# One transformer block on one core: the search for the order of its operations takes another seed and 73 rounds for 110

## The chip, the cores and the metric

The kernel runs on one core of one Trainium2 chip. That core has five engines that work side by side, each through its own list of instructions in order: TensorE (PE in the profile, with PEld for its weight loads), VectorE (DVE), ScalarE (ACT), GpSimd (POOL) and SyncE (SP), which here issues the DMA transfers. An instruction waits until what it reads has been written and what it overwrites has been read.

The metric is the time of one execution on the device in microseconds (us), the median of several runs. All times below are us from the start of the profiled span unless they say otherwise.

## The reference, cut to what matters

One sequence of 2048 tokens with 448 features goes through one block: layer norm, attention with 16 heads of 28 in a sliding window of 256 tokens, a residual addition, layer norm, a gated feed-forward part of width 1792, and a second residual addition.

```python
h = x + attention(layernorm(x))          # 16 heads, Dh 28
    # q, k, v = split(y @ wqkv);  p = softmax(mask(q @ k.T * 28 ** -0.5)), 0 <= i - j < 256
    # (p @ v) @ wo
h2 = h + (gelu(y @ w_gate) * (y @ w_up)) @ w_down      # y = layernorm(h), width 1792
return h2                                               # all float32
```

## The kernel before, in words

**Numbers.** Products in float32 are made from two parts: the high part of a value (`to_hi`, line 498, an ACT copy into the matmul type) and the rest (`to_lo`, line 501, a subtraction on DVE or POOL). A projection, a value product or a feed-forward convolution is then a sum of hi x hi, hi x lo and lo x hi. So nearly every matmul has line 495 (the helper `mul`); which one it is, the names of its operands and its width tell.

**Stages.** Tokens are cut into 16 tiles of 128 and 4 chunks of 512. The heads are worked on in two passes of 8. In each pass and chunk the kernel makes

- values: 11 matmuls of width 224 per tile (`bank<-proj,xT 128x224`), evicted by ACT;
- projections of queries and keys: 11 matmuls of width 512 per weight tile (`bank<-xT,proj 128x512`); their result goes to DRAM and comes back into `ring` in the layout of the scores;
- two blocks of four heads and 512 queries, 16 in all. A block has 16 scores (`bank<-ring` 84x384, one per head and query tile); DVE takes the masked row maximum of each from its PSUM bank (line 924, tile `mt`); for each half of the block one small matmul (line 951, `one,mhl`) turns the maxima, which ACT writes beside the queries; then 24 probability matmuls (`bank<-ring` 104x128 to 104x384) give the scores again, transposed and with the maximum subtracted, and ACT takes the exponential out of the bank (line 996, tile `pp`); POOL clears what lies outside the window (line 1007). Two attention groups per block (line 1026, twelve matmuls each, recorded as 24, `bank<-pp,v`) multiply by the values; 32 of them in all;
- the output projection: 24 matmuls per chunk (`bank<-wos,ohl 128x448`), added to the residual `hres` by DVE (line 1073).

The feed-forward part starts with eight plain convolution steps (line 1320 issues them; the first two, 'early', are made while attention still runs and have the form `bank<-xT,proj 128x512` too), and goes on with 24 steps in a scheme of seven products each (`unit`), whose operands POOL and DVE form (line 693 and line 1164). Each step is followed by a down projection into four banks, which DVE adds to `hres` (line 1296). Weight records for it come in by DMA (line 1157, `raw<-in_halves`) and are split into `proj` or `ring`. The transposed operands go by way of small transfers (line 674, `v<-xn`).

**Banks.** PSUM has eight banks. Two take scores, two probabilities, two are the attention accumulators, and the last two take values, projections and output products, and scores or probabilities once the projections are done (`allowed`, line 1533). A matmul into a bank waits until the engine that evicts it is through with the result before.

**What sets the order.** Nothing is issued as it is written. Each operation is recorded by `op` with its engine, an assumed cost, a latency, a key, and what it reads and writes. `run` (line 140) then plays the lists through: at each step it takes, among the operations that are ready on an engine, the one with the lowest key that can begin soonest, gives it a bank if it needs one, and so forms one list per engine. Where PE would have nothing in the first 26 us, `idle` puts a transpose of the identity there (line 1571).

Before that, `refine` (line 337) changes the keys. It draws from a random generator with a fixed seed. In each round it either sets all keys from the latest times at which the operations could run without delaying the end (`latest`, line 290), mixed with their present times and with noise, or shifts the operations of one kind in one stretch. Then it plays the lists anew and values the order with

```python
return 1e9 if s is None else 0.4 * s + 0.3 * sum(self.replay(random.Random(i)) for i in (1, 2))
```

where `s` is the end by the assumed costs and `replay` (line 252) plays the fixed order with costs that are longer at random. A better order is kept, a worse one with a probability that falls. The keys of the best order found are those that are used:

```python
L.refine(allowed, idle)
L.run(allowed, idle, True)
```

Of the kernel before, what the change touches and what calls it, by code (L numbers as in the profile page):

```python
# [72 lines left out]
    return max(n / 2400 + 0.004, 0.112)  # L73


ROUNDS = 110
SEED = 3
HEAT = 0.3
MIX = 0.8
COOL = 800  # L80
# [16 lines left out]
class Lists:  # L97
# [239 lines left out]
    def refine(self, allowed, idle):  # L337

        rnd = random.Random(SEED)

# [5 lines left out]
        kept = keys = [o.key for o in self.ops]  # L346
        for r in range(ROUNDS):
            kind = rnd.random()
# [1285 lines left out]
```

## Time and profile before

| what | value |
|---|---|
| median of 3 runs | 686.99 us (686.92 to 687.37) |
| the profiled execution | 687.41 us |
| its span | 685.70 us, so 1.71 us lie around it |
| mean granted clock of TensorE | 0.998 |
| starts of attention groups 22 to 32 | 230.08, 239.57, 248.45, 258.52, 266.00, 273.71, 286.00, 292.87, 304.17, 311.02, 319.36 |
| share of the span on the chain of work that ended last | PE 86%, DVE 7%, ACT 3%, DMA 3% |

A row of the timeline has the start, the length, the engine, the line, the operation and its operands (destination <- sources, partitions x elements), and a count where like instructions were joined; what stands in brackets is the idle time ahead of it and what ended that. A row of the windows has the stretch, its length, then for PE, PEld, DVE, ACT and POOL the busy time and the number of instructions, and at the end the granted clock (1.00 is full speed), the share of the DMA engines' time that was busy, and GB/s. Matmuls overlap their neighbours, so the distance from one start to the next is shorter than a recorded length.

### The profile page before, as it was taken

The page shows a single profiled execution, that of the slowest core. Times are in us where ns is not written, and L with a number is a line of the kernel's source. Part 1 is how long each engine was busy: PE and PEld are TensorE (multiplying, and loading weights), DVE is VectorE, ACT ScalarE, POOL GpSimd, SP SyncE. Part 2 cuts the span into 40 slices and gives each one's busy share as a digit, 9 for nine tenths or more (in the row PEclk, how much of TensorE's full clock was granted, in tenths as well). Part 3 has the DMA queues.
Part 4 walks back from the last instruction along what each step waited for, and adds up shares of the span by engine and source line. Part 5 has one row for each costly group of instructions (what it writes and reads, how often), then busy time and mean ns, then how long its engine had stood idle before and what let it go on. Part 6 is the DMA issues. An engine that isn't in the chain of part 4 may idle for free.

```text
span 685.7 us, 12258 instructions
## 1 busy us (share of the span) xinstructions
PE 673.9 (98%) x4079; PEld 593.4 (87%) x4079; DVE 502.4 (73%) x1274; ACT 419.6 (61%) x908; POOL 296.8 (43%) x462
## 2 busy tenths in 40 slices
PE   8999999999999999999999999999999999999997
PEld 8898888888888877677898899899999999999997
DVE  7968978866587867784899998877667745645544
ACT  7758767777766789696655665644554543533331
POOL 5702544344445668546524465254664631501100
PEclk9999999999999999999999999999999999999999
DMA  8798765566547687633533432212212210111102
GB/s 290 229 307 264 225 186 177 165 191 197 174 149 221 171 245 195 168 74 85 148 91 101 116 110 75 86 53 76 66 53 90 67 53 14 39 53 67 54 1 107
DMA packets 92951, 89.67 MB, mean 131 GB/s; under 512 B 35224, under 2 KB 82008, under 8 KB 92888
## 3 DMA queue, kind: packets, MB, share of 16 engines
q1 hardware_dynamic: 92888, 88.89, 43.4%
q8 instruction: 32, 0.52, 0.3%
q14 instruction: 31, 0.25, 0.1%
HBM read 59.51 MB, written 29.36 MB: 130 GB/s over the span
## 4 chain that ended last, share of the span: by engine, by line
PE 86%; DVE 7%; ACT 3%; DMA 3%; issue 1%; POOL 0%; SPq 0%; DVEq 0%; ACTq 0%
PE bank L495 79%; PE bank L1026 6%; DMA v<-xn 1%; ACT ring L498 1%; PE bank L553 1%; DVE proj L501 1%; DVE v L693 1%; DVE X L501 1%; DVE mt L924 1%; DVE hres L1296 1%; DMA q<-proj 1%; ACT proj L498 1%; ACT xT L498 1%; ACT pp L996 1%; DVE bnst L530 0%
## 5 line engine op out<-in xcount | busy, mean ns | idle before, releaser
L495 PE MATMUL bank<-xT,proj 128*128 128x512 f32 x620 | 178.9, 387 | 0.0
L495 PE MATMUL bank<-ring 84*128 84x384 f32 (+5 forms) x618 | 155.4, 314 | 2.6 <-ACT pp L996 1.5
L924 DVE CUSTOM_DVE_ANT_0 mt<-bank,mt 128x384 bf16<-128x384 f32 (+2 forms) x256 | 129.0, 526 | 36.9 <-PE bank L495 31.9
L996 ACT ACTIVATE pp<-bank 128x384 f32<-128x384 f32 (+2 forms) x352 | 123.6, 390 | 45.1 <-PE bank L495 41.7
L495 PE MATMUL bank<-xT,ring 128*128 128x512 f32 x536 | 134.9, 380 | 0.1
L495 PEld LDWEIGHTS bank<-ring 104*128 104x128 f32 (+2 forms) x618 | 109.8, 191 | 25.6 <-issue 5.6
L495 PE MATMUL bank<-ring,proj 128*128 128x448 f32 x628 | 127.5, 353 | 1.6 <-DVE hres L1296 1.6
L1007 POOL TENSOR_SCALAR_AFFINE_SELECT pp<-pp 128x512 f32<-128x512 f32 x120 | 74.9, 638 | 117.2 <-ACT pp L996 106.1
L495 PEld LDWEIGHTS bank<-xT,proj 128*128 128x128 f32 x620 | 114.4, 191 | 10.8 <-issue 0.6
L495 PEld LDWEIGHTS bank<-ring,proj 128*128 128x128 f32 x628 | 118.6, 189 | 4.6 <-ACT xT L498 1.9
L495 PEld LDWEIGHTS bank<-xT,ring 128*128 128x128 f32 x536 | 100.9, 189 | 13.5 <-DVE v L1240 0.5
L1296 DVE TENSOR_TENSOR hres<-bank,hres 128x448 f32<-128x448 f32 x72 | 41.3, 622 | 26.8 <-PE bank L495 26.7
L495 PE MATMUL bank<-proj,xT 128*128 128x224 f32 x352 | 59.9, 275 | 0.2 <-ACT proj L498 0.2
L1258 ACT ACTIVATE v<-v 128x512 f32<-128x512 f32 x24 | 15.2, 632 | 69.5 <-DVE v L1240 69.5
L501 POOL TENSOR_TENSOR ring<-raw,ring 128x256 fp32r<-128x256 f32 (+2 forms) x42 | 38.3, 921 | 42.1 <-ACT ring L498 34.3
L495 PEld LDWEIGHTS bank<-proj,xT 128*128 128x128 f32 x352 | 53.2, 191 | 1.5 <-ACT proj L498 0.4
L1164 POOL TENSOR_TENSOR v<-raw 128x256 f32<-128x256 f32 x18 | 15.4, 856 | 89.8 <-DMA raw<-in_halves_dram 54.9
L495 PE MATMUL bank<-wos,ohl 128*128 128x448 f32 x192 | 50.2, 363 | 0.0
L501 DVE TENSOR_TENSOR proj<-v,proj 128x512 fp32r<-128x512 f32 (+1 forms) x56 | 43.0, 773 | 8.6 <-ACT proj L498 7.4
L498 ACT ACTIVATE proj<-v 128x512 fp32r<-128x512 f32 (+1 forms) x56 | 33.6, 603 | 24.3 <-DVE v L1266 13.4
L495 PE MATMUL bank<-X,ring 128*128 128x512 f32 x146 | 48.2, 379 | 0.0
L1164 POOL TENSOR_TENSOR raw<-raw 64x128 f32<-64x128 f32 (+1 forms) x90 | 46.1, 525 | 2.2
(116 smaller groups left out, 987.5 us busy)
## 6 DMA issues: line engine op xcount, KB each, us to landing
ring<-k SPq DMA_DIRECT2D x44, 336.0 KB
raw<-in_halves_dram SPq DMA_DIRECT2D x18, 640.0 KB
ring<-q SPq DMA_DIRECT2D x32, 336.0 KB
q<-proj SPq DMA_DIRECT2D x15, 448.0 KB
k<-proj SPq DMA_DIRECT2D x11, 448.0 KB
hres<-in_x_dram SPq DMA_DIRECT2D x16, 224.0 KB
xn<-xn SPq DMA_DIRECT2D x64, 56.0 KB
mt<-in_halves_dram SPq DMA_DIRECT2D x16, 224.0 KB
```

Of the source, the lines that this page charges most:

```text
L495: nc.tensor.matmul(o.rearrange("p (t h) -> p t h", h=2), w, mixed(m), **how)
L498: nc.scalar.activation(dst, src, AF.Copy)
L501: (eng or nc.vector).tensor_sub(dst, src, f(hi))
L553: nc.tensor.transpose(bank[b.k][:, n * 128:(n + 1) * 128], xn[i2][:, o:o + 128], ident)
L693: op("dve", 0.07 + n * 0.00104, 0.17 + n * 0.00104, key, lambda: nc.vector.tensor_tensor(out, a, b, op=op_), [*ar, *br, "mtfree"], w, port ...
L924: nc.vector.tensor_tensor_reduce(plain(junk[s % 2][:, o:384]), unmixed(bank[b.k][:, o:384]), plain(mask[:, o:384]), 1.0, -BIG, OP.add, OP. ...
L996: nc.scalar.activation(plain(pp[:, j, o * 128:o * 128 + n]), unmixed(bank[b.k][:, 0:n]), AF.Exp, scale=SCALE)
L1007: nc.gpsimd.affine_select(a, a, pattern=[[0, 4], [-cm, 128]], compare_op=op_, fill=0.0, base=0, channel_multiplier=cm)
L1026: nc.tensor.matmul(bank[b.k][32 * j:32 * j + DH + 1, lo * 128:(hi + 1) * 128], v[:, 4 * c - 2 + m, g % 2, j, :], pp[:, j, at[m] * 128:(at[ ...
L1164: op("pool", 0.14 + n * 0.00215, 0.18 + n * 0.00215, key, lambda: nc.gpsimd.tensor_tensor(out, a, b, op=OP.subtract), [*ar, *br], w, port= ...
L1258: op("act", 0.485, 0.608, key + 11, lambda: nc.scalar.activation(A, A, AF.Gelu_apprx_tanh), ta, ta)
L1296: op("dve", 0.533, 0.626, key + 3 * q + 3, lambda t=t, b=banks[q]: nc.vector.tensor_tensor(plain(hres[:, t, :]), unmixed(bank[b.k][:, 0:D] ...
```

## The change

Two constants of the search differ:

```diff
-ROUNDS = 110
-SEED = 3
+ROUNDS = 73
+SEED = 13
 HEAT = 0.3
 MIX = 0.8
 COOL = 800
```

The operations, their operands, their costs and what depends on what are the same. What differs is the random sequence, so other keys are tried, and the order that comes out is another. The warming transposes go from 35 to 38. PE's list differs up to the matmul that stands at 329.10 in the profile before, and is the same from there to the end (1696 operations); DVE and ACT differ up to about 440, POOL and SP up to about 500.

Three places show it. The names `bank_138` to `bank_145` are the eight PSUM banks: 138 and 139 take scores (384 wide), 140 and 141 probabilities, 142 and 143 are the accumulators of attention, 144 and 145 the two shared ones.

The first place is PE behind attention group 25. Before, from the fourth row behind the group on:

```order
L495 MATMUL bank_144<-wos,ohl 128x448
L495 MATMUL bank_145<-ring 128x256
L495 MATMUL bank_144<-wos,ohl 128x448
L951 MATMUL bank_141<-one,mhl_156 72x128
L495 MATMUL bank_144<-wos,ohl 128x448
L495 MATMUL bank_138<-ring 128x384
L495 MATMUL bank_140<-ring 128x128
L495 MATMUL bank_144<-wos,ohl 128x448
L495 MATMUL bank_139<-ring 128x384
L495 MATMUL bank_145<-ring 128x256
```

And now, from the first row behind the same group:

```order
L495 MATMUL bank_140<-ring 128x256
L495 MATMUL bank_144<-wos,ohl 128x448
L495 MATMUL bank_141<-ring 128x256
L495 MATMUL bank_144<-wos,ohl 128x448 x4
L495 MATMUL bank_140<-ring 128x256
L495 MATMUL bank_144<-wos,ohl 128x448
L495 MATMUL bank_141<-ring 128x256
L495 MATMUL bank_145<-ring 128x128
L495 MATMUL bank_138<-ring 128x384
L495 MATMUL bank_140<-ring 128x128
L495 MATMUL bank_141<-ring 128x128
L495 MATMUL bank_144<-wos,ohl 128x448 x6
```

Between groups 25 and 26 the output matmuls (`wos,ohl`) were 12 and are 24 now, all four tiles of the chunk, and two value matmuls stand there too. The scores in this stretch were 6 and there is 1. Counted over all from group 22 to group 32, value matmuls were 54 and are 66, projections 28 and 33, output matmuls 48 and 53; scores 63 and 62; probabilities (115), early convolutions (71) and turned maxima (9) are as many as before.

The second place is PE and ACT behind attention group 27. PE before, from the end of the group on:

```order
L1026 MATMUL bank_143<-pp,v 29x384 x4
L495 MATMUL bank_138<-ring 128x384
L495 MATMUL bank_139<-ring 128x384
L495 MATMUL bank_140<-ring 128x256
L495 MATMUL bank_141<-ring 128x256
L495 MATMUL bank_145<-ring 128x128
L495 MATMUL bank_140<-ring 128x256
L495 MATMUL bank_141<-ring 128x128
L495 MATMUL bank_138<-ring 128x384
```

PE now:

```order
L1026 MATMUL bank_143<-pp,v 29x384 x4
L495 MATMUL bank_140<-ring 128x384
L495 MATMUL bank_138<-ring 128x384
L495 MATMUL bank_141<-ring 128x256
L495 MATMUL bank_139<-ring 128x384
L495 MATMUL bank_145<-ring 128x256
L495 MATMUL bank_140<-ring 128x256
L495 MATMUL bank_138<-ring 128x384
L495 MATMUL bank_141<-ring 128x256
L495 MATMUL bank_145<-ring 128x384
```

ACT in the same place now:

```order
L498 ACTIVATE v<-bank_144 128x8x28
L498 ACTIVATE ohl<-oT 128x512
L498 ACTIVATE proj<-raw 128x512 x2
L996 ACTIVATE pp<-bank_140 128x384
L996 ACTIVATE pp<-bank_141 128x256
L996 ACTIVATE pp<-bank_145 128x256
L498 ACTIVATE xT<-xT 128x3x128
L498 ACTIVATE ring<-xT 64x128
L498 ACTIVATE xT<-xT 64x128
L996 ACTIVATE pp<-bank_140 128x256
L996 ACTIVATE pp<-bank_141 128x256
L498 ACTIVATE proj<-raw 128x448
```

Behind the group 17 scores and probabilities stand ahead of the first early convolution before and now, in another sequence. On ACT three splits of a weight record (`proj<-raw`) now stand between this group and the next, where there was none before.

The third place is DVE at the second group of four residual additions of the feed-forward part (line 1296; PE takes the same four banks again behind them). Before:

```order
L693 TENSOR_TENSOR v<-v 128x128
L1341 TENSOR_TENSOR mt<-bank_139,mt 128x512
L1296 TENSOR_TENSOR hres<-bank_142,hres 128x448
L1296 TENSOR_TENSOR hres<-bank_143,hres 128x448
L1296 TENSOR_TENSOR hres<-bank_144,hres 128x448
L1296 TENSOR_TENSOR hres<-bank_145,hres 128x448
```

Now:

```order
L501 TENSOR_TENSOR proj<-raw,proj 128x2x128 x2
L1296 TENSOR_TENSOR hres<-bank_142,hres 128x448
L1296 TENSOR_TENSOR hres<-bank_143,hres 128x448
L1296 TENSOR_TENSOR hres<-bank_144,hres 128x448
L1296 TENSOR_TENSOR hres<-bank_145,hres 128x448
L1341 TENSOR_TENSOR mt<-bank_139,mt 128x512
```

The product with the gate (line 1341) has gone behind the four additions, and one more split (line 501) stands ahead of them. On SP the load of a weight record (line 1157) that stood ahead of a run of transfers `v<-xn` stands behind three of them now.

## The prediction

> **What bounds the kernel now.** I read the page's head, the waits of PE, the busy time by stage, the same table between attention groups, and last the timeline of single places. The page first:
>
> ```profile
> span 685.7 us, 12258 instructions
> PE 673.9 (98%) x4079; PEld 593.4 (87%) x4079; DVE 502.4 (73%) x1274; ACT 419.6 (61%) x908; POOL 296.8 (43%) x462
> ```
> PE (TensorE) is busy for all but 11.8 us of the span. A new order leaves the matmuls as they are, so it can only take waits out or put waits in. The waits that PE's engine shows (engine, line, waited for; total, times, longest):
>
> ```profile
> PE bank L495 <- DVE proj L501: 1.7, 1, 1.7
> PE bank L495 <- DVE hres L1296: 1.6, 1, 1.6
> PE bank L495 <- ACT pp L996: 1.5, 4, 0.8
> PE bank L495 <- DVE mx L924: 0.6, 2, 0.4
> ```
> Two are single places; the others are small and belong to one stretch. The table by stage (start:end, length, then busy us of PE, PEld, DVE, ACT, POOL with counts, granted clock, DMA) shows which:
>
> ```profile
> 12.00:25.00 13.00, 13.00 (x82) 11.70 (x81) 12.45 (x31) 12.34 (x23) 8.83 (x23) 1.00 0.66 230
> 25.00:230.08 205.08, 205.03 (x1553) 176.28 (x1551) 160.68 (x552) 146.56 (x366) 85.41 (x120) 1.00 0.67 206
> 230.08:319.36 89.28, 86.64 (x630) 67.92 (x629) 64.81 (x205) 75.22 (x196) 57.62 (x86) 0.98 0.64 160
> 331.10:365.40 34.30, 32.71 (x160) 30.02 (x160) 31.13 (x84) 19.54 (x35) 11.19 (x20) 1.00 0.40 109
> 398.80:680.40 281.60, 281.60 (x1372) 259.04 (x1373) 183.32 (x310) 131.45 (x234) 102.73 (x160) 1.00 0.19 59
> ```
> From 12 to 230.08 us and from 398.80 to 680.40 us PE never lets go for more than 0.05 us in all. The waits stand in 230.08:319.36 (attention groups 22 to 32), where the clock is below 1 as well, and at the two handovers behind it. Busy time hides part of a wait, since a matmul's recorded time overlaps the next one's; so I price matmuls by the distance of their starts:
>
> ```profile
> 249.86 0.81 PE L495 MATMUL bank<-ring 84*128 84x384 f32 x4
> 250.51 1.03 PE L495 MATMUL bank<-xT,proj 128*128 128x512 f32 x4
> 251.38 0.28 PE L495 MATMUL bank<-ring 104*128 104x256 f32 x1
> 251.49 0.23 PE L951 MATMUL bank<-one,mhl 128*72 128x128 f32 x1
> ...
> 251.77 0.48 PE L495 MATMUL bank<-proj,xT 128*128 128x224 f32 x3
> 252.09 0.34 PE L495 MATMUL bank<-ring 84*128 84x384 f32 x1
> ...
> 273.71 1.50 PE L1026 MATMUL bank<-pp,v 128*29 128x128 f32 x24
> 275.14 0.88 PE L495 MATMUL bank<-ring 84*128 84x384 f32 x5
> ...
> 324.56 4.70 PE L495 MATMUL bank<-wos,ohl 128*128 128x448 f32 x24
> 329.10 0.35 PE L495 MATMUL bank<-proj 128*128 128x448 f32 x1
> ```
> A score of 384 columns costs 0.65/4 = 0.16 us, a projection or early conv of 512 0.87/4 = 0.22, a probability of 256 0.11 (0.06 for 128 by halving; 0.11 on the average of a block's 24), a value matmul 0.32/3 = 0.11, an output matmul 4.54/24 = 0.19. An attention group takes 1.43 us (273.71 to 275.14), and I allow 0.5 us for its start and end (an estimate: with it the sums below come out at no wait for the stretches where PE's row is full).
>
> **The stretch with the waits.** One row from each group to the next:
>
> ```profile
> 239.57:248.45 8.88, 8.77 (x77) 7.33 (x77) 4.88 (x17) 7.83 (x23) 5.78 (x8) 1.00 0.89 250
> 248.45:258.52 10.07, 9.32 (x76) 7.76 (x75) 7.48 (x24) 8.30 (x22) 6.19 (x9) 1.00 0.89 245
> 258.52:266.00 7.48, 7.22 (x56) 5.36 (x55) 5.79 (x22) 6.39 (x20) 5.15 (x7) 1.00 0.94 242
> 266.00:273.71 7.71, 7.53 (x55) 5.55 (x54) 5.56 (x16) 7.16 (x19) 7.22 (x13) 1.00 0.62 152
> 273.71:286.00 12.29, 11.24 (x69) 8.20 (x69) 9.40 (x37) 7.68 (x23) 7.45 (x12) 0.86 0.83 215
> 286.00:292.87 6.87, 6.87 (x55) 5.15 (x54) 5.99 (x19) 5.72 (x14) 3.69 (x6) 1.00 0.31 67
> ```
> With the order's counts at the prices above, PE's own work from group 27 to group 28 (273.71:286.00) is 7.7 us (the group, 13 scores, 16 probabilities, 11 early convs, one maximum); with the 0.5 us around the group 4.1 us are waits. The same sum gives 1.6 us for 248.45:258.52, 0.9 for 258.52:266.00, 0.7 for 266.00:273.71 and for 239.57:248.45, 0 for 286.00:292.87, and 0.8 us for the stretches not shown: 8.8 us for the ten from group 22 to group 32. What the 4.1 us are:
>
> ```profile
> 276.32 0.60 PE L495 MATMUL bank<-ring 104*128 104x256 f32 x2 [0.30 <-ACT pp L996]
> 277.31 1.63 PE L495 MATMUL bank<-ring 84*128 84x384 f32 x6 [0.40 <-DVE mx L924]
> 279.17 0.91 PE L495 MATMUL bank<-ring 84*128 84x384 f32 x3 [0.22 <-DVE mx L924]
> 279.91 1.44 PE L495 MATMUL bank<-xT,proj 128*128 128x512 f32 x4
> ...
> 281.00:282.00 1.00, 1.00 (x4) 0.76 (x3) 0.26 (x2) 0.50 (x1) 0.91 (x3) 0.50 0.98 275
> ...
> L924 DVE CUSTOM_DVE_ANT_0 mt<-bank,mt 128x384 bf16<-128x384 f32 (+2 forms) x256 | 129.0, 526 | 36.9 <-PE bank L495 31.9
> ```
> Behind group 27 stand 17 scores and probabilities without any filler (a matmul that waits for no bank of the block); they take 4.77 us for 2.4 us of work, since each score needs 0.53 us of DVE before its bank comes back. Then the clock falls to 0.50, which costs the other 1.7 us or so.
>
> **Term 1, the fillers, -1.8 us.** From group 22 to group 32 the new order has 12 value, 5 projection and 5 output matmuls more (66, 33, 53 against 54, 28, 48) and as many scores, probabilities and early convs: 12 x 0.11 + 5 x 0.22 + 5 x 0.19 = 3.4 us of work that stood ahead of group 22, where PE did not wait. So group 22 comes 3.4 us earlier, the work behind it is 3.4 us more, and only the waits count. Groups 25 to 26: 26 fillers in place of 12, so that 0.9 falls to 0.2. Groups 26 to 27: 20 for 12, but of the shorter kind; 0.7 falls to 0.2. Groups 24 to 25: 22 for 26, and the last ten in front of the group are scores, probabilities and a maximum; five scores take 2.6 us of DVE beside 1.3 us of PE, of which half may be covered: 1.6 falls to 0.9 (ends 0 and 1.6). Groups 27 to 28: again 17 small matmuls before the first early conv; 4.1 stays, the half-speed clock with it (ends 2.4 without it and 5.8 with a second one). The rest stays. The sum of waits is 6.9 us in place of 8.8 (the shares rounded to -1.8).
>
> [...]
>
> **Term 2, the handovers, -0.3 us.** At 365.4 PE waits for the four residual additions that give the down banks back:
>
> ```profile
> 364.02 0.68 DVE L1341 TENSOR_TENSOR mt<-bank,mt 128x512 f32<-128x512 f32 x1
> 364.63 2.20 DVE L1296 TENSOR_TENSOR hres<-bank,hres 128x448 f32<-128x448 f32 x4
> ```
> The new order puts the 0.6 us of L1341 behind them and a split of 0.33 us ahead: the additions come 0.27 us earlier. What is late next is that L1341, whose result the down group two steps on reads, some 7 us later. At 331.1 PE waits 1.7 us for the low part of the first conv product. In the run of DVE in front of it the same four additions, three products and one statistic stand in another order, and one transpose of 0.64 us has left it, which lay ahead of a wait:
>
> ```profile
> 325.89 0.62 DVE L1073 TENSOR_TENSOR hres<-bank,hres 128x448 f32<-128x448 f32 x1 [0.48 <-PE bank L495]
> ```
> I take 0 (ends -0.6 and +0.6, one operation either way).
>
> **Term 3, the rest, +0.1 us.** From 329.1 us on PE's own order is the same to the end. DVE, ACT and SP change up to 500 us, under 281.60 us in which DVE is busy for 183.32: this cover holds unless one result comes late by more than its margin. The largest move is on SP:
>
> ```profile
> 363.10 0.36 SPq L1157 DMA_DIRECT2D raw<-in_halves_dram  x1
> 363.51 7.41 SPq L674 DMA_DIRECT2D v<-xn  x6
> ...
> 377.39 0.41 DVE L501 TENSOR_TENSOR ring<-raw,ring 128x256 fp32r<-128x256 f32 x1
> ...
> 379.49 1.03 PE L495 MATMUL bank<-xT,ring 128*128 128x512 f32 x4
> ```
> The weight record's load now stands behind three of those six, up to some 4 us later (363.51 and half of 7.41, against 363.10). Its last split ended at 377.80, and PE reads it from the third matmul of the row at 379.49, 379.9: a margin of 2.1 us. Ends 0 and +2; I take 0.1, nearest the rows without a wait. At the start three more warming transposes (38 for 35) fill waits and cost nothing; the first projection is bound by the same DVE work up to about 14 us, and from 12 us on the table shows no wait (ends -0.5 and +0.5).
>
> The sum is -2.0 us. The profiled execution took 687.41 us (span 685.70 and 1.71 around it), 0.42 above the median of 686.99; against the median the forecast is 685.0 us.
>
> **The rivals.** [...] (b) No gain: the pace in groups 24 to 28 is set by the chain score, maximum, probability, exponential, and fillers only shift the waits: 687.0. For it: no engine is full there (DVE 7.48 of 10.07, ACT 8.30). (c) Slower: ACT sets the pace. Between groups 24 and 28 the new order gives ACT 30.0 us up to the last exponential needed, against 27.5, and three weight splits of 0.6 us stand between the exponentials for group 28. For it: ACT is 7.16 of 7.71 busy in 266.00:273.71 and ended four waits. Then this stretch takes 37.6 + 2.5 us, from a start 2.0 us earlier, PE has 0.6 us more to do behind group 28, so +1.1; a second half-speed stretch brings +1.7, and terms 2 and 3 -0.2: 689.6. It decides where ACT falls over 2 us behind PE at group 28. Against it: ACT had room of 4.6 us in 273.71:286.00. That the order stays as it was is excluded: it differs on every engine.
>
> **How the numbers follow.** 0.2% is 1.4 us, about what a measurement of this kernel can tell from no change. Forecast 0.45, own range 683.9 to 686.2, of which 0.36 is faster and 0.09 within; (a) 0.14, faster; (b) 0.14, within; (c) and like losses in the reordered FFN 0.27, slower. So 0.50 faster, 0.23 the same, 0.27 slower. The range 682.6 to 689.9 takes in (a) and (c) and leaves out some 0.05 below (both of 24 to 25's wait and the clock) and 0.13 above (more than one stretch of (c)).
>
> **What would show it.** Term 1: groups 25 to 27 each within 0.5 us of their work, group 22 near 227 us, 27 to 28 near 12 us with a row at clock 0.50. Term 2: the wait on L1296 at 1.3 us. Term 3: no wait of PE behind 370 us. It is wrong if waits on ACT pp L996 exceed 2 us in all, if a second row at 0.50 appears, or if PE waits between 25 and 230 us, where the old order had none.

## The result and the profile after

| kernel | median of the runs | lowest to highest | mean granted clock |
|---|---|---|---|
| before (4 runs) | 687.10 us | 686.92 to 687.37 | 0.998 in the profiled execution |
| after (4 runs) | 690.67 us | 689.51 to 691.69 | 0.993 to 0.998 |

The change makes the kernel slower: the ratio is 1.0058, with a 95% interval of 1.0040 to 1.0075. The forecast was 685.0 us, so it misses by 5.7 us, and the sign is wrong.

The page of the kernel after (its profiled execution took 689.51 us):

```profile
span 687.8 us, 12274 instructions
PE 675.3 (98%) x4082; PEld 592.5 (86%) x4082; DVE 506.6 (74%) x1274; ACT 419.7 (61%) x908; POOL 298.6 (43%) x462
```
The waits of PE after (engine, line, waited for; total us, times, longest):

```profile
PE bank L495 <- ACT pp L996: 2.1, 5, 0.8
PE bank L495 <- DVE proj L501: 1.9, 1, 1.9
...
PE bank L495 <- DVE mx L924: 0.6, 2, 0.3
...
PE bank L495 <- DVE pp L501: 0.5, 1, 0.5
```
The wait on the residual additions (L1296, 1.6 us before) is gone in this execution. A wait on DVE's split of a projection (`pp L501`) is new, and the waits on ACT's exponentials have grown from 1.5 to 2.1 us. The stages after (start:end, length, busy us of PE, PEld, DVE, ACT, POOL, granted clock, DMA share, GB/s):

```profile
12.00:25.00 13.00, 13.00 (x77) 11.62 (x77) 12.40 (x31) 10.18 (x18) 8.40 (x19) 1.00 0.82 274
25.00:230.46 205.46, 204.44 (x1536) 172.55 (x1535) 159.69 (x547) 147.08 (x364) 85.14 (x121) 1.00 0.65 202
230.46:322.97 92.51, 89.19 (x652) 70.94 (x651) 67.98 (x211) 77.79 (x198) 58.46 (x89) 0.98 0.61 157
...
402.00:684.00 282.00, 281.74 (x1373) 258.87 (x1371) 187.08 (x311) 131.18 (x234) 103.31 (x158) 1.00 0.19 60
```
The second row is the one to look at. It ends where attention group 22 starts, at 230.46 us. The old order reached that group at 230.08 us, with some 3.3 us more PE work done by then. So the new order takes 0.4 us longer for less work, at full clock: PE stands still for 1.0 us there, against 0.05 before, and busy time hides more.

To see all of it, I price every matmul by the prediction's rows and add up by how much the distance from each start to the next exceeds the price. Up to 240 us the sum is 3.5 us higher after than before: 1.3 us of this arises between 20 and 40 us, 1.6 between 160 and 180, and the other 0.6 is spread. The windows of these places, before and then after:

```profile
24.00:30.00 6.00, 6.00 (x37) 5.42 (x36) 5.80 (x14) 3.35 (x7) 5.36 (x8) 1.00 0.82 241
160.00:180.00 20.00, 20.00 (x159) 17.26 (x157) 13.84 (x55) 14.30 (x39) 7.88 (x11) 1.00 0.56 175
```

```profile
24.00:30.00 6.00, 5.53 (x44) 5.17 (x43) 5.82 (x13) 3.71 (x8) 5.27 (x8) 1.00 0.95 298
160.00:180.00 20.00, 19.65 (x154) 15.48 (x144) 13.23 (x49) 12.96 (x33) 8.73 (x13) 1.00 0.48 138
```
The timeline after shows what PE waits for in the two places (start, length, engine, line, operation, in brackets the idle time ahead and its releaser):

```profile
24.10 2.26 POOL L794 MEMSET ring<- 32x1024 f32 x2
...
25.39 1.39 DVE L800 CAST ring<-e 8x768 fp32r<-8x768 f32 x1
...
27.35 0.67 DVE L501 TENSOR_TENSOR pp<-bank,pp 128x512 fp32r<-128x512 f32 x1
...
28.08 1.48 PE L495 MATMUL bank<-proj,xT 128*128 128x224 f32 x11 [0.47 <-DVE pp L501]
...
173.76 1.27 POOL L501 TENSOR_TENSOR ohl<-oT,ohl 128x512 fp32r<-128x512 f32 x1 [0.28 <-ACT ohl L498]
...
174.04 1.02 DVE L944 SCALAR_TENSOR_TENSOR mhl<-mx,mhl 128x8 fp32r<-128x8 f32 x1
...
175.58 0.91 PE L495 MATMUL bank<-ring 84*128 84x384 f32 x3 [0.29 <-DVE mx L924]
```
In both places a small DVE operation takes several times its usual length beside a long POOL operation, and the DVE work that PE waits for is queued behind it. L944 works on 8 elements per partition; the median of its 32 times is 0.166 us, here it takes 1.02 us and ends at 175.06, when POOL's subtraction ends (175.03). The L800 copies take 0.56 us in the old order; this one takes 1.39 us, beside the second MEMSET, which runs up to 26.36. That MEMSET in turn takes 1.37 us, where the first takes 0.95: it starts beside the first copy.

The two long DVE operations end 0.03 and 0.42 us behind the POOL operation beside them. Of the 64 L944 of the two traces nine take over 0.3 us (0.32 to 1.03; five before, four after). Each of the nine starts while a POOL operation of line 501 or 1007 runs, and ends some 0.02 us behind one. Where POOL's subtraction starts 0.06 to 0.15 us after the L944, the L944 takes 0.16 to 0.17 us (87.42 and 205.56 us before, 88.52 and 191.35 after). Why, no run shows. Two of the long ones in the old order, 1.03 us at 80.15 and 1.01 at 104.62, fall in a stretch in which PE lacks 0.05 us in all.

Last, the stretch that the prediction was about. Between attention groups after:

```profile
249.34:259.91 10.57, 10.12 (x73) 8.03 (x72) 8.14 (x28) 9.08 (x23) 7.30 (x9) 1.00 0.83 232
259.91:268.99 9.08, 8.65 (x67) 7.35 (x66) 6.72 (x20) 6.94 (x22) 5.89 (x9) 1.00 0.80 200
268.99:275.45 6.46, 6.46 (x61) 5.42 (x60) 5.75 (x18) 6.03 (x14) 5.23 (x12) 1.00 0.96 260
275.45:287.54 12.09, 11.20 (x64) 7.84 (x63) 7.64 (x29) 8.80 (x27) 9.34 (x11) 0.86 0.78 194
306.32:315.15 8.83, 7.59 (x56) 5.74 (x55) 6.45 (x16) 8.60 (x21) 4.58 (x9) 1.00 0.26 58
284.00:285.00 1.00, 1.00 (x5) 0.91 (x4) 1.00 (x2) 0.49 (x2) 1.00 (x2) 0.50 0.91 318
```
The waits between groups, by one sum for both traces (length less work at the prices, less 0.5 us around a group). Here every matmul has the price of its own width; so the old order comes to 9.7 us where the prediction, with average prices, had 8.8:

| groups | 22-23 | 23-24 | 24-25 | 25-26 | 26-27 | 27-28 | 28-29 | 29-30 | 30-31 | 31-32 | all |
|---|---|---|---|---|---|---|---|---|---|---|---|
| before | -0.1 | 0.8 | 1.3 | 1.3 | 0.8 | 4.4 | 0.0 | 0.8 | 0.4 | 0.0 | 9.7 |
| after | -0.1 | 0.1 | 1.3 | 1.0 | -0.2 | 4.8 | 0.3 | 1.1 | 1.3 | -0.1 | 9.7 |

So the fillers (matmuls that wait for no bank of the block) moved the waits and did not remove them. The stretch is 3.2 us longer, as much as the work that came into it.

### The profile page after: what moved, and what is told of

Same layout as the page of the kernel before. It is cut to its first block, busy times and chain, and to the rows that moved or that the text cites. A ratio compares the mean times of both kernels' runs of the same rounds, so it can differ in the third digit from the quotient of the medians.

```text
span 687.8 us, 12274 instructions
## 1 busy us (share of the span) xinstructions
PE 675.3 (98%) x4082; PEld 592.5 (86%) x4082; DVE 506.6 (74%) x1274; ACT 419.7 (61%) x908; POOL 298.6 (43%) x462
## 4 chain that ended last, share of the span: by engine, by line
PE 86%; DVE 6%; DMA 3%; ACT 3%; issue 1%; SPq 1%; POOL 0%; DVEq 0%; ACTq 0%
PE bank L495 79%; PE bank L1026 5%; DMA xT<-xn 1%; DMA xn<-xn 1%; DVE proj L501 1%; DMA q<-proj 1%; DVE mt L924 1%; PE bank L553 1%; DVE xT L501 1%; ACT ring L498 1%; ACT pp L996 1%; DVE bnst L530 0%; ACT xn L548 0%; DVE hres L1073 0%; PE bank L951 0%
## 5 line engine op out<-in xcount | busy, mean ns | idle before, releaser
L495 PE MATMUL bank<-xT,proj 128*128 128x512 f32 x620 | 175.8, 386 | 0.0
L495 PE MATMUL bank<-ring 84*128 84x384 f32 (+6 forms) x618 | 156.2, 314 | 3.5 <-ACT pp L996 2.1
L996 ACT ACTIVATE pp<-bank 128x384 f32<-128x384 f32 (+2 forms) x352 | 125.3, 389 | 46.7 <-PE bank L495 39.7
L1296 DVE TENSOR_TENSOR hres<-bank,hres 128x448 f32<-128x448 f32 x72 | 41.5, 623 | 27.8 <-PE bank L495 27.8
L501 POOL TENSOR_TENSOR ring<-raw,ring 128x256 fp32r<-128x256 f32 (+2 forms) x42 | 37.8, 907 | 39.7 <-ACT ring L498 37.8
L495 PEld LDWEIGHTS bank<-proj,xT 128*128 128x128 f32 x352 | 51.4, 191 | 1.9 <-DVE pp L501 0.6
L501 DVE TENSOR_TENSOR proj<-v,proj 128x512 fp32r<-128x512 f32 (+1 forms) x56 | 45.5, 817 | 9.7 <-ACT proj L498 8.3
L1164 POOL TENSOR_TENSOR raw<-raw 64x128 f32<-64x128 f32 (+1 forms) x90 | 48.5, 552 | 2.1
```

Of the source, the lines that this page charges most:

```text
L495: nc.tensor.matmul(o.rearrange("p (t h) -> p t h", h=2), w, mixed(m), **how)
L501: (eng or nc.vector).tensor_sub(dst, src, f(hi))
L996: nc.scalar.activation(plain(pp[:, j, o * 128:o * 128 + n]), unmixed(bank[b.k][:, 0:n]), AF.Exp, scale=SCALE)
L1164: op("pool", 0.14 + n * 0.00215, 0.18 + n * 0.00215, key, lambda: nc.gpsimd.tensor_tensor(out, a, b, op=OP.subtract), [*ar, *br], w, port= ...
L1296: op("dve", 0.533, 0.626, key + 3 * q + 3, lambda t=t, b=banks[q]: nc.vector.tensor_tensor(plain(hres[:, t, :]), unmixed(bank[b.k][:, 0:D] ...
```

## The experiments

Each experiment issues a prescribed order in place of the one that the search would set, with all operations kept. The common edit, at lines 1575 and 1576:

```diff
-    L.refine(allowed, idle)
-    L.run(allowed, idle, True)
+    keys = [o.key for o in L.ops]
+    follow(L, chosen(L.ops, lambda seed, rounds: search(L, keys, allowed, idle, seed, rounds)), allowed, idle)
```
`search` runs `refine` with a seed and a number of rounds and gives back the order found; `follow` plays every engine's list in that order. Only `chosen` differs from kernel to kernel. "Old" is the order of seed 3 with 110 rounds, "new" that of seed 13 with 73. (Built with seed 13 and 110 rounds, the kernel is the same program, so of the two constants only the seed matters here.)

An execution's mean granted clock gives an estimate of how many stretches at half clock it had: the one in the profile before, of 3.41 us (280.39 to 283.81) in a span of 685.70, lowers the mean by 0.0025, to 0.998. The old kernel beside these experiments took 684.4 to 686.2 us at a mean of 1.000 (14 runs), 686.7 to 688.3 at 0.998, and 690.3 to 690.6 at 0.992. So part of a difference between medians is the number of these stretches, and below I compare at equal clock where it decides. The mean alone doesn't set the time: at 0.996 the old kernel took 686.0 to 686.6 us, less than at 0.998. Where a stretch falls seems to matter too; that was not followed up.

### Which half of the order it is

**Old order ahead of attention group 15, new behind it, and the reverse.** Group 15 starts at 174.4 us in the old order.

```diff
+def chosen(ops, found):
+    one, two = found(3, 110), found(13, 73)          # e2: found(13, 73), found(3, 110)
+    cut = [t for o, t in one if o.tag == "att"][14]
+    done = [o for o, t in one if t < cut]
+    return done + [o for o, t in two if o not in set(done)]
```

> The order of before up to the start of attention group 15 (174.41 us), the new order for all that is left. Theory F (front): the new order loses its time where PE seemed to wait for nothing, at 20 to 40 us (1.3 us) and at 160 to 180 us, and takes back up to 1.8 us at the handover at 365 us because DVE comes there on its own time. Then this kernel saves most of the loss: PE some 2.5 us earlier than the new order at group 15, some 1 to 2 us earlier at the end, 687.0 to 689.0 us. Theory B (behind group 24): the loss lies behind group 24, in the stretches where ACT sets the pace and in half-speed stretches; then it is as slow as the new order, 690 to 691 us.

> The new order up to the start of attention group 15 (177.91 us there), the order of before for all that is left. Theory F: PE is 2.5 to 3 us late at group 15, and the wait of 1.7 us at 365 us takes 1 to 1.8 us of that back: 688.0 to 689.0 us, with the wait on line 1296 under 0.7 us. Theory B: as before, 687.0 us.

Measured: with the old front 689.06 us (12 runs), 1.0014 [0.9997, 1.0032] of the kernel before; with the new front 690.45 us (8 runs), 1.0053 [1.0032, 1.0075]. At a mean clock of 1.000 the new front takes 689.1 to 689.9 us, some 3.3 us more than the old order at that clock.

In the trace of the old front with the new back, group 22 starts at 227.04 us, and it ran three stretches at half clock where the kernel after had one:

```profile
281.00:282.00 1.00, 1.00 (x5) 0.82 (x4) 0.93 (x4) 0.21 (x2) 1.00 (x1) 0.50 0.63 186
284.50:285.50 1.00, 1.00 (x4) 0.82 (x3) 0.00 (x0) 0.10 (x1) 0.00 (x0) 0.50 0.69 117
335.50:336.50 1.00, 1.00 (x5) 0.89 (x4) 1.00 (x3) 0.00 (x0) 0.92 (x2) 0.50 1.04 207
```
What follows: the loss is in the front. Theory B fails in both kernels; theory F had the direction, but both medians lie above its ranges, by 0.1 and 1.5 us. Whether the back gains is not to be read here, since the half clock covers it (mean 0.994 over the 12 runs).

### The wait at 365 us

**The move of L1341 alone, in the old order, and undone in the new one.**

```diff
+    # e3, in the old order: the product with the gate (L1341) behind the second four additions (L1296)
+    dve[i - 1:i + 4] = dve[i:i + 4] + dve[i - 1:i]
+    # e4, in the new order: ahead of them again
+    dve[i:i + 5] = dve[i + 4:i + 5] + dve[i:i + 4]
```

> The order of before, and only DVE's product with the gate (line 1341) goes behind the four additions at 365 us. Theory A (absorbed): the additions come one product of 0.61 us earlier, the wait of 1.6 us falls to 1.0 us, and the time by 0.6 us to 686.5 us; the rest of the 1.7 us that the new order does not wait there is PE coming later. Theory S (the swap carries it): the wait goes as in the new order, 685.4 us.

> The new order, and only DVE's product with the gate goes ahead of the four additions again. Theory A: the additions come 0.6 us later, which is about the 0.5 us by which they were early for PE: 0 to 0.2 us more than the new order, 689.5 to 691.7 us, wait on line 1296 under 0.3 us. Theory S: the wait of 1.6 us is back, some 692 us.

Measured: 687.13 us for the move alone (12 runs), 1.0000 [0.9988, 1.0012]; 692.34 us for the new order without it (6 runs), 1.0069 [1.0051, 1.0088]. At a mean clock of 1.000 the move alone took 685.4 to 685.8 us, the kernel before 685.1 to 686.2: about 0.2 us less, which three runs against six do not tell from nothing. The fourth kernel had more half clock than the kernel after (mean 0.995, two such stretches in its trace), so its 1.7 us over the kernel after aren't the price of the move.

DVE's timeline with the move alone, and then its waits of PE:

```profile
363.12 2.20 DVE L1296 TENSOR_TENSOR hres<-bank,hres 128x448 f32<-128x448 f32 x4
365.25 0.67 DVE L1341 TENSOR_TENSOR mt<-bank,mt 128x512 f32<-128x512 f32 x1
```

```profile
PE bank L495 <- DVE proj L501: 1.7, 1, 1.7
...
PE bank L495 <- DVE v L1240: 0.7, 1, 0.7
```
And the additions' wait in the new order without the move:

```profile
371.02 2.51 PE L495 MATMUL bank<-ring,proj 128*128 128x448 f32 x12 [1.01 <-DVE hres L1296]
```
What follows: in this trace the additions start at 363.12 in place of 364.63, 1.5 us earlier, and the whole wait of 1.58 us is gone. But only 0.6 us of this is the move, one product, as theory A had it. The other 0.9 us arise some 25 us ahead of it, in the same order. There ACT splits a weight record as soon as its load has landed, and DVE's work up to the additions hangs on it (a split of DVE at 361.58 us before stands at 360.68 with the move). The load was issued at 332.92 us before and at 332.90 with the move; the split before, with the move, and in the kernel after (load issued at 336.26):

```profile
338.96 0.63 ACT L498 ACTIVATE proj<-raw 128x512 fp32r<-128x512 f32 x1 [1.72 <-DMA raw<-in_halves_dram]
```

```profile
338.04 0.63 ACT L498 ACTIVATE proj<-raw 128x512 fp32r<-128x512 f32 x1 [0.82 <-DMA raw<-in_halves_dram]
```

```profile
340.44 0.63 ACT L498 ACTIVATE proj<-raw 128x512 fp32r<-128x512 f32 x1 [0.67 <-DMA raw<-in_halves_dram]
```
From issue to split that is 6.0, 5.1 and 4.2 us, and the wait on L1296 is 1.6, 0 and 0. Undone in the new order, a wait of 1.0 us is there, but there the load took 5.2 us, so this is not the price of the move either. So the two theories are not decided by these waits. Little of what is gained reaches the end: PE comes sooner to work that waits for DVE anyway, and a wait of 0.7 us on the gelu's input (`v L1240`) opens at 398 us. That PE's lateness had closed the wait by itself falls: with the new front and the old back (the second experiment) PE comes there 2.7 us later than in the old order, the load is issued as much later, and PE still waits 0.8 us, with 5.4 us from issue to split. The old order's row, and that of the second experiment:

```profile
365.38 2.51 PE L495 MATMUL bank<-ring,proj 128*128 128x448 f32 x12 [1.58 <-DVE hres L1296]
```

```profile
367.33 2.51 PE L495 MATMUL bank<-ring,proj 128*128 128x448 f32 x12 [0.78 <-DVE hres L1296]
```

### Whether the loss in the front is one place or two

```diff
+    cut = [t for o, t in one if o.tag == "att"][7]      # old order up to group 8, new behind it
```

> The order of before up to the start of attention group 8 (112.6 us), the new order for all that is left. The new order lost 3.2 us ahead of group 15 by the runs with the order exchanged there. Theory two places: 1.3 us of it stand at 20 to 40 us and 1.6 us at 160 to 180 us, each on its own; then this kernel saves the first and keeps the second: some 1.3 us under the new order, 688.2 us where the mean clock is 0.998. Rival: the later loss follows from the order of the first 60 us; then all is saved, 686.3 us at clock 0.998, as with the order exchanged at group 15.

Measured: 688.83 us (11 runs), 1.0018 [1.0007, 1.0030]; in its trace the loss between 20 and 40 us is gone, that between 160 and 180 us stays, at 1.3 us over the old order. So they are two places, and the one doesn't bring about the other. In time the first saves more than the 1.3 us expected: the two runs at a mean clock of 0.998 took 687.5 and 687.6 us, and the theory had 688.2.

### Half clock taken away

**The old order, the new one, and old front with new back, each with transposes of the identity in PE's gaps from 240 to 400 us.** They go only into an attention accumulator bank that is idle, nothing reads them, and nothing of the computation is left out. The old order gets 57 more matmuls, the new one and the mix 59 each.

```diff
+WARMED = 240, 400
...
+            warm = WARMED[0] < free["pe"] < WARMED[1]
+            WARM = 1e9 if warm else 26.0
+            until = idle(free["pe"], t, {k: bank_free[k] if k in (4, 5) else None for k in bank_free}
+                         if warm else bank_free, True)
```

> The order of before, with transposes of the identity into an idle accumulator bank put where PE's list has gaps between 240 and 400 us (some 60, as at the start of the kernel). Theory G: the clock of the next 3.41 us is halved where the array was used by less than about 0.39 over the last 3.41 us (0.374 and 0.363 were followed by half speed, 0.402 and 0.425 were not); behind attention group 27 the order of before is at that edge. Then the mean clock is 1.000 in nearly every run and the median is that of the runs of before with clock 1.000, 685.9 us, with a narrower spread. [...]

> The new order with the same transposes in its gaps. Theory G: clock 0.999 to 1.000, and what is left of the difference to before is the front: 688.3 to 689.0 us, that is 2.4 to 3.0 us over the order of before with transposes. [...]

> The order of before up to the start of attention group 15, the new order behind it, and the transposes in the gaps between 240 and 400 us. Theory front plus G: the front of before saves 3.2 us, the back of the new order is 0.8 us better than that of before at full clock, and the half-speed stretches (three in most runs of the same order without transposes) are gone: 685.0 to 685.5 us, clock 1.000, faster than both kernels. [...]

| order with transposes | median (runs) | ratio to before | mean clock |
|---|---|---|---|
| old | 686.02 us (11) | 0.9979 [0.9964, 0.9994] | 0.999 to 1.000 |
| new | 689.48 us (7) | 1.0032 [1.0019, 1.0044] | 0.999 to 1.000 |
| old to group 15, new behind | 684.94 us (6) | 0.9965 [0.9952, 0.9978] | 0.999 to 1.000 |

The page and the waits on L1296 of the mix:

```profile
span 683.1 us, 12389 instructions
PE 674.5 (99%) x4138; PEld 597.3 (87%) x4138; DVE 507.2 (74%) x1274; ACT 419.7 (61%) x908; POOL 298.6 (44%) x462
```

```profile
PE bank L495 <- DVE hres L1296: 0.4, 1, 0.4
```
Theory G had the clocks right in all three, and the times to within 0.5 us (the new order is 0.5 us above its range, the mix 0.1 below). What follows, now that little differs but the order: the new order costs 3.46 us (689.48 - 686.02). With the new back behind it, its front, up to group 15, costs 4.54 (689.48 - 684.94); behind the old front, its back gains 1.08 (686.02 - 684.94). In the traces of the old order and the mix 0.6 us of that gain is the wait on L1296 (1.0 with the old back); the group waits by the sum above differ by 0.2. The two shares depend on which half is exchanged first: with the old back the new front costs 3.3 us (the second experiment at a mean clock of 1.000), and behind the new front the new back then gains nothing (689.2 with the old back, 689.48 with the new). So the front costs 3.3 to 4.5 us and the back gains at most 1.1. The mix is faster than both kernels, by 2.2 us against the one before.

### What the stalls beside POOL are worth

**The new order with the transposes and two DVE operations moved**: L944 behind the next two maxima, and the second L800 copy behind the split at 27.35 us that PE waits for.

```diff
+    move(order, minus, most[1], True)                # line 944 at 174.04 us
+    return move(order, ops[78], ops[197], True)      # line 800, the second copy
```
The new order as it was ran beside it once more (the gate's edge in its expectation is the 0.39 of theory G).

> The new order with the transposes of the identity in its gaps (so that the clock stays at 1.000), and two moves on DVE alone: the subtraction of line 944, which took 1.02 us at 174.04 us beside a subtraction of POOL (173.76 to 175.03 us) and 0.16 us elsewhere, goes behind the next two maxima; the second copy of line 800, which took 1.39 us at 25.39 us beside a POOL memset and 0.56 us elsewhere, goes behind the split of line 501 that PE waited for at 28.08 us. Theory contention: two of the front's waits (0.64 us at 28.08, 0.46 and 0.23 us at 174 to 176 us) come from DVE operations that stand still beside POOL; they go, and the time is 1.0 to 1.3 us under the same order without the moves, 688.2 to 688.5 us. Rival clumps: the waits come from like matmuls standing together on PE and only change their name: 689.5 us.

> The new order as it is, once more, beside the run above on the same chip, for the share of the half-speed stretches: mean clock 0.9955 against 0.997 of before if its back half is nearer to the gate's edge; median 690.2 to 691.2 us, and 689.3 to 689.7 us in the runs with clock 0.998. If its clock is that of before, 0.997, the half-speed stretches are no part of the difference.

Measured: 688.08 us with the two moves (12 runs, 1.0017 [1.0004, 1.0031]), against 689.48 without them; the kernel after once more 689.99 us (7 runs, 1.0062 [1.0038, 1.0087]). DVE's timeline with the moves:

```profile
26.74 0.56 DVE L800 CAST ring<-e 8x768 fp32r<-8x768 f32 x1
```

```profile
174.52 0.19 DVE L944 SCALAR_TENSOR_TENSOR mhl<-mx,mhl 128x8 fp32r<-128x8 f32 x1
```
Both operations have their usual length again, and the two waits of PE (0.47 at 28.08, 0.29 at 175.58) are gone. So the two long DVE operations (1.02 us for 0.17, 1.39 for 0.56) are 1.0 to 1.4 of the 4.54 us that the front costs. The medians differ by 1.4, but the two kernels ran on different chips, with the kernel before at 687.53 and 687.16 us beside them, so up to 0.4 us may be the chip. In the two traces group 22 starts 1.0 us earlier with the moves (229.41 against 230.42), and the end comes 1.0 us earlier, although a wait of 0.49 us for a transfer of queries has opened at 149.02; so the rival, that waits only change their name, is not excluded for a part. In the repeat of the kernel after, the first of the two copies is the long one (1.45 us, the second 0.56), and PE waits 0.18 us behind them.

The rest of the front, about 3 us, is not settled. In the traces with transposes group 22 starts 3.8 us later with the new front than with the old one and the same back (230.42 against 226.60), with the same matmuls ahead of it but for three warming transposes, and the end comes 4.2 us later. What the traces show there beside the two places are waits of about 0.2 us on DVE and ACT, and none was tried by itself.

## Why the prediction was wrong

- **Term 1, the shift: the step that failed.** "work that stood ahead of group 22, where PE did not wait. So group 22 comes 3.4 us earlier". The count of fillers was right: behind the old front, the new back has group 22 at 227.04 us, 3.0 us earlier (with transposes in both, 3.5). But behind its own front it has it at 230.46. Term 3 held the same assumption, "from 12 us on the table shows no wait (ends -0.5 and +0.5)". The row 25.00:230.08 with PE at 205.03 of 205.08 showed the old order there, and I took its lack of waits for a property of the stretch. DVE was 160.68 busy of 205.08 and the operations there were reordered on every engine, so there was no ground for a bound of 0.5. This step costs 4.54 us of the miss of 5.7, or 3.3 if the halves are exchanged in the other order; 1.0 to 1.4 us of it are two DVE operations that took 1.02 and 1.39 us beside POOL, for 0.17 and 0.56 elsewhere, and what makes up the rest stays open. The prediction's own sign of being wrong, that PE waits between 25 and 230 us, came true with 1.0 us.
- **Term 1, the waits, -1.8.** (Its three shares add up to -1.9.) Right for groups 26 to 27 (forecast 0.2, measured none); wrong for 24 to 25 (forecast 0.9, measured 1.3 in both orders) and mostly for 25 to 26 (forecast 0.2, measured 1.0). What was gained came back as waits further on, most in 30 to 31. In all the term is 0.0 in the profiles, and -0.2 between the old order and the mix with transposes. For this term rival (b) was right: fillers shift the waits.
- **27 to 28 stays, with its half clock.** Right: 12.09 us and a row at 0.50, as forecast. The 0.14 of (a) stood for no stretch at half clock and 683.3 us. No run of the new order without transposes shows it: the profile after has the stretch from 282.97 us (280.39 before), and none of these eleven runs had a mean clock over 0.998.
- **Rival (c), ACT sets the pace between 24 and 28, a second stretch at half clock.** It gave 689.6, close to the time, but not for the reason: 24 to 28 has no more waits than before (6.9 against 7.8 us by the table). The mechanism shows elsewhere, at 306.32:315.15, where ACT is busy for 8.60 of 8.83 us and PE waits 1.2 us for its exponentials, 0.9 more by the table than the old order lost there. This is also why the waits on L996 exceed the 2 us named as a refutation.
- **Term 2, -0.3.** Near in the time, wrong in the trace: the wait was to stay at 1.3 us and is gone in the profile after. The path was another than the one priced: the additions stand at the end of work that begins with the split of a weight record, and this came 4.2 us behind the issue of its load, for 6.0 before; from the split to the additions it is 26.0 us, for 25.7, so the 0.27 us are not to be seen. With transposes the wait is 1.0 us in the old order and 0.4 to 0.6 in the three kernels with the new back. In the eight traces with the new back the split stands 4.2 to 5.2 us behind the issue, in the four with the old one 5.1 to 6.0; why is not settled. The move alone gave about 0.2 us in time, within the spread. At the first handover the forecast of 0 (ends -0.6 and +0.6) holds: 1.7 us before, 1.9 after.
- **Term 3 behind 370 us.** Right: PE lacks 0.26 us in 402:684, and the load of the weight record that SP issues later delays nothing.
- **The half clock.** The forecast let it cost both orders the same, and the runs don't contradict this: with transposes the old order falls by 0.0021 of 687.53, 1.4 us, and the new one by 690.67 - 689.48 = 1.2, or 0.5 by the 689.99 of the repeat. The new order does have more of it, as the last expectation had it: its eleven runs have a mean clock of 0.995 on average, the 67 of the old order beside the experiments 0.997. Whether it loses more time to it isn't settled.

Added up with transposes: +4.54 where 0 stood, -1.08 where -2.1 stood for terms 1 and 2, which makes +3.46; the medians differ by 3.57. The range ended at 689.9, 0.8 us short: its upper end took in a slower back and losses in the reordered feed-forward part, and no loss ahead of group 22.

## What to carry to other kernels

That an engine never waits in a stretch is a property of the order that was measured; when a search reorders the other engines there, price the stretch with ends on both sides as large as the waits seen elsewhere. In a new order look for short DVE operations that now start beside a long POOL operation, ahead of something that the bound engine waits for (here one took 1.02 us for 0.17, one 1.39 for 0.56). Where executions differ in granted clock, compare orders at equal clock, or fill the bound engine's gaps with harmless matmuls first; here that alone gave the old order 1.4 us.

## What the runs showed of the hardware that was not expected

**The half clock came behind windows of low use.** In the traces of the two kernels the changes of clock fall on a grid of 3.41 us: at 7.33, 280.39 and 283.81 us before (80 steps of 3.413 us, and one), at 6.49, 282.97 and 286.38 after (81, and one). So it does not begin at the same time in both. For each window of such a grid in the twelve traces, from 12 us on and ahead of the one in which the matmuls end, I sum the streaming time of its matmuls (0.42 ns a column, from the 0.87 us that four of 512 take), each weighted by the share of the 128 x 128 array it uses (84 x 128 for a score), over 3.41 us. The matmuls of an attention group start in fours 7 ns apart, and two rounds of 256 columns start 0.216 us apart (249.10 and 249.31 us before), so I count four side by side, at twice the time a column. These are my sums from the traces, not counters. Eleven windows were followed by half clock: 0.376 (before), 0.252 (after), 0.221, 0.366 and 0.397 (old front with new back), 0.338 (third experiment), 0.216 and 0.351 (fourth), 0.254 and 0.378 (fifth), 0.298 (the repeat of the kernel after). Of the other 2339 windows in the twelve traces the lowest have 0.388 (second experiment), 0.400 (fourth), 0.413 (fifth) and 0.427 (two of the kernels with transposes). So by these sums the edge lies near 0.40 here, with one window on the wrong side, and a second one at the end of the kernel after: the window in which its matmuls end (682.32 to 685.74 us) has 0.366, and the clock behind it stays at 1.00 to the end of the span. The edge was fitted afterwards, to these traces alone. The longest wait of PE near these stretches was 0.5 us near 280 us (0.4 before, 0.3 after, 0.3 in the first experiment, 0.5 in the fourth) and 1.9 us near 334 us (first experiment).

**With transposes of 128 columns in the gaps the clock stayed at 0.999 to 1.000.** Some 57 of them in 160 us brought the mean clock of 36 runs of four kernels to 0.999 or 1.000, where the three orders that also ran without them had 0.992 to 1.000. The times then vary less: the 11 runs of the old order spread over 1.9 us, where 24 without transposes beside them spread over 5.3.
